# Scale sums in 64 columns and one bank, scaled rows on two engines, and the first tile's row products ahead of the constants' rows

## The chip, the cores and the metric

The kernel runs on one core of one Trainium2 chip. The metric is the device time of one execution in microseconds (us); lower is better. The engines are called PE (matrix products), PEld (its weight loads), DVE (vector), ACT (activation), POOL (GpSimd) and SP (which issues most of the transfers here). PSUM is the memory that PE writes; the kernel cuts it into banks of 128 partitions by 512 fp32 numbers.

## The reference

One block of a spectral network on x of 2048 rows by 512 columns. The condition c gives six rows of 512 (`sa, ca, ga, sb, cb, gb`). The first half normalizes x, scales it by 1+ca, shifts it by sa, filters it in the frequency domain and adds it back; the second half does the same around two dense layers with a Mish between.

```python
mod = (_silu(c) @ w_mod).reshape(c.shape[0], 6, 1, -1)
sa, ca, ga, sb, cb, gb = (mod[:, 0], mod[:, 1], mod[:, 2], mod[:, 3], mod[:, 4], mod[:, 5])
h = _layernorm(x, axis=-1) * (1 + ca) + sa
x = x + ga * _A_ref(h, A_w_r, A_w_i)    # irfft2(rfft2(h) * (w_r + 1j*w_i))
h = _layernorm(x, axis=-1) * (1 + cb) + sb
x = x + gb * _B_ref(h, B_w1, B_b1, B_w2)    # mish(h @ w1 + b1) @ w2
```

## The kernel before

The transform is written as matrix products with constant matrices. x is cut into 16 tiles of 128 rows. The first stage, which the change touches, runs over these tiles n = 0 to 15 and takes about the first 49 us:

- `p1_row(n)`, the row products: four matmuls of the turned tile (`xring`, x with rows and columns exchanged, loaded by `load_xt`) with `krs`, the constant matrix `kr` whose rows are multiplied by 1+ca. So krs carries the scale of the norm, and no row product can start before ca is known.
- `row_sums()`: the same four matmuls with a matrix of ones instead of x. Their result, copied by ACT to `kb`, is what a row's mean has to be multiplied with. These are the constants' rows of the title.
- `norm_sums(n)` on DVE reads the tile itself (`x`, loaded by `load_x`) and gives mean and variance; `first_guess` on ACT (an Ln, L188, and an Exp, L189) and `first_scale` on DVE (three small instructions, L196) make 1/sqrt(variance) of them.
- `p1_mean(n)` on DVE (L284) takes mean times kb from the row products; `p1_cast` on ACT (L300 or L294) scales the result and rounds it to `gh`; `p1_low` on DVE (L307) makes the rest `gl` for even n (POOL does it for odd n).
- `p1_col(n)`: nine matmuls (three times L314, L315, L316) with `mring`, the column matrices that ACT and POOL split from `mraw` (`p1_split`, loaded by `load_m`). The last three of them take gl.

Ahead of this stands the prologue. `sc` is silu(c), spread over partitions. `scale_sums` makes ca: 16 matmuls, four steps k by four column blocks j, each with a 128x128 block of `wmc` (the part of w_mod for ca, loaded in four transfers, one for each k) as weights and one column of sc, repeated, as the moving operand. Each fp32 matmul runs as two passes, each with its weight load, so 16 matmuls show as 32 rows of PE and of PEld. Block j adds up in its own bank `ps[j]`, all columns of it alike. `scale_rows` is one DVE instruction for each block: krs[j] = kr[j] * ps[j] + kr[j]. A few matmuls on ones (`warm`, L355) run before the first load has landed.

In this stretch everything is issued in the order in which it is written (`manual_schedule`); each engine works through its own queue in that order, and waits on semaphores for the others. SP issues the loads one by one in the order written; with eight lanes, the ninth load waits until the first has landed, and so on. The later stages (spectral products, way back, dense layers in seven products in the order of a table) follow unchanged.

```python
def row_products(pg, data):                                          # L266
    pgv = pg.rearrange("p (c d q) -> p d c q", c=2, d=4)
    for j in range(4):
        nc.tensor.matmul(pgv[:, j], data(j), krs[:, j, :].rearrange("p (c q) -> p c q", c=2),
                         start=True, stop=True)                      # L269

def row_sums():                                                      # L277
    ps = bank("D")
    row_products(ps, lambda j: ones)
    nc.scalar.copy(kb, ps)                                           # L280

def p1_mean(n):                                                      # L282
    c = st.pop(("pg", n))
    nc.vector.scalar_tensor_tensor(c, kb, mv[:, n, 0:1], c, op0=ALU.mult, op1=ALU.subtract)
    st["c", n] = c
```

Of the kernel before, what the change touches and what calls it, by code (L numbers as in the profile page):

```python
# [7 lines left out]
F32 = mybir.dt.float32  # L8
F32R = mybir.dt.float32r
AF = mybir.ActivationFunctionType  # L10
ALU = mybir.AluOpType

P = 128
# [70 lines left out]
def tile_spectral_block(ctx: ExitStack, tc: tile.TileContext, x_d, w1_d, b1_d, w2_d,  # L84
                        c_d, xt_d, wm_d, wq_d, wz_d, kr_d, km_d, kc_d, ki_d, kf_d, kv_d, kw_d, kp_d, out_d):
    nc = tc.nc
# [4 lines left out]
    small = ctx.enter_context(tc.tile_pool(name="small", bufs=4))  # L91
# [21 lines left out]
    def bank(tag):  # L113
        return psum.tile([P, 512], F32, name="bank", tag=tag)
# [8 lines left out]
    def buf(tag, dt=F32):  # L123
        if tag in "ty":
            uses[tag] = uses.get(tag, 1) + 1
            return wide(tag)[:, uses[tag] % 2]
        return work.tile([P, 512], dt, name="buf", tag=tag)

    def plain(t):
        return t.bitcast(F32)  # L130

    x = base.tile([P, N2, D], F32, name="x")
    sc = base.tile([P, 4], F32, name="sc")
# [6 lines left out]
    krs = modr[:, 0].rearrange("p (j e) -> p j e", j=4)  # L140
# [11 lines left out]
    wmc = big.tile([P, 4, 512], F32, name="wmc", tag="cr")  # L152
# [8 lines left out]
    kr = pw.tile([P, 4, P], F32, name="kr")  # L161
# [6 lines left out]
    def scale_spread():  # L168
        ps = bank("D")
        for k in range(4):  # L170
            nc.tensor.matmul(ps[:, k * P:(k + 1) * P], sc[:, k:k + 1].to_broadcast([P, P]), ident,
                             start=True, stop=True)
        st["scb"] = ps
# [7 lines left out]
    def norm_sums(n):  # L181
        t = small.tile([P, 6], F32, name="st")
        nc.vector.bn_stats(t, x[:, n, :])
        nc.vector.bn_aggr(mv[:, n, :], t)
# [6 lines left out]
    def norm_refine(lo, hi, sign, r=None):  # L191
        r = rstd[:, lo:hi] if r is None else r
        t = small.tile([P, 4], F32, name="ve")[:, 0:hi - lo]
        for out, a, one, op in ((t, mv[:, lo:hi, 1], EPS, ALU.add), (t, t, -0.5 * sign, ALU.mult),
                                (rstd[:, lo:hi], t, 1.5 * sign, ALU.add)):
            nc.vector.scalar_tensor_tensor(out, a, one, r, op0=op, op1=ALU.mult)  # L196

    def first_guess(lo, hi):
        st["r", lo] = r = bank("D")[:, 0:hi - lo]
        norm_guess(lo, hi, r)  # L200

    def first_scale(lo, hi):
        norm_refine(lo, hi, -1, st.pop(("r", lo)))
# [27 lines left out]
    def load_m(n):  # L231
        nc.sync.dma_start(mraw[:, n, :], km_d[:, n, :])

    def load_x(n):
        nc.sync.dma_start(x[:, n:n + 1, :], xv[:, n:n + 1, :])

    def load_xt(n):
        t = xring[:, n % 8]
        nc.sync.dma_start(t, xt_d[n])
        st["xt", n] = t  # L240

    def load_all(n):
        load_xt(n)
        load_x(n)
        load_m(n)
# [13 lines left out]
    def p1_split(n):  # L259
        m = mt(n)  # L260
        nc.scalar.copy(m[:, 0, 0:256], mraw[:, n, :])
        nc.gpsimd.tensor_tensor(m[:, 1, 0:256], mraw[:, n, :], plain(m[:, 0, 0:256]), op=ALU.subtract)
        nc.gpsimd.tensor_scalar(m[:, :, 256:384], plain(m[:, :, 128:256]), -1.0, 0.0,
                                op0=ALU.mult, op1=ALU.add)
# [7 lines that stand above are left out]
    def p1_row(n):  # L272
        xt = st.pop(("xt", n))
        st["pg", n] = pg = bank("AB"[n % 2])
        row_products(pg, lambda j: xt[:, j, :])
# [11 lines that stand above are left out]
    def p1_cast(n):  # L287
        c = st["c", n]
        one = rstd[:, n:n + 1]
        gh, gl = buf("g1", F32R), buf("g2", F32R)  # L290
        if n in POOL_LOW:
            g = buf("t")
            if n == 1:
                nc.scalar.activation(gh, c, AF.Copy, scale=one)  # L294
            nc.scalar.activation(g, c, AF.Copy, scale=one)
            if n > 1:
                nc.scalar.copy(gh, g)
            nc.gpsimd.tensor_tensor(gl, g, plain(gh), op=ALU.subtract)
        else:
            nc.scalar.activation(gh, c, AF.Copy, scale=one)  # L300
        st["g", n] = gh, gl
# [17 lines left out]
    def p1_save(n):  # L319
        nc.scalar.copy(a_sb[:, :, n, :], st.pop(("pa", n)).rearrange("p (e q) -> p q e", e=8))  # L320

    def scale_sums(ks, ps):
        for k in ks:
            for j in range(4):
                nc.tensor.matmul(ps[j][:, 0:P], wmc[:, k, j * P:(j + 1) * P], sc[:, k:k + 1].to_broadcast([P, P]),  # L325
                                 start=(k == 0), stop=(k == 3))

    def scale_rows(ps):
        for j in range(4):
            nc.vector.scalar_tensor_tensor(krs[:, j, :], kr[:, j, :], ps[j][:, 0:1], kr[:, j, :],  # L330
                                           op0=ALU.mult, op1=ALU.add)

    def shift_sum(k):
        mod_column(wms[:, k, :], cols[:, 0, 0, k:k + 1], 128.0, bank("D"))
# [17 lines left out]
    def warm(count, tag="B"):  # L352
        ps = bank(tag)
        for _ in range(count):
            nc.tensor.matmul(ps[:, 0:P], ones, ones, start=True, stop=True)  # L355

    with tc.manual_schedule():
        nc.sync.dma_start(sc, c_d.rearrange("b (p k) -> p (b k)", k=4))
        nc.scalar.preload_act_table_set("natural_log_exp_and_others")
        for k in range(4):  # L360
            nc.sync.dma_start(wmc[:, k, :], wm_d[1, k])
        nc.sync.dma_start(kr, kr_d)
        load_x(0)
        load_xt(0)
        nc.sync.dma_start(ident, kp_d)
        load_xt(1)
        load_m(0)
        for n in range(1, 8):
            load_x(n)
            if n < 7:  # L370
                load_xt(n + 1)
            load_m(n)
        nc.vector.memset(ones, 1.0)
        nc.vector.memset(eps, EPS)
        nc.vector.memset(b1n[:, NF - 1:NF], 0.0)
        sg = small.tile([P, 4], F32, name="sg")
        nc.scalar.activation(sg, sc, AF.Exp, scale=-1.0)
        nc.vector.tensor_scalar(sg, sg, 1.0, None, op0=ALU.add)
        nc.vector.reciprocal(sg, sg)
        nc.vector.tensor_tensor(sc, sc, sg, op=ALU.mult)  # L380
        warm(6)
        cps = [bank(t) for t in "CCBB"]
        for k in range(4):
            scale_sums((k,), cps)
        scale_rows(cps)
        row_sums()
        norm_sums(0)
        first_guess(0, 1)
        first_scale(0, 1)
        p1_split(0)  # L390
        p1_row(0)
        load_all(8)
        p1_row(1)
        load_all(9)
        scale_spread()
        p1_mean(0)
        p1_cast(0)
        norm_sums(1)
        first_guess(1, 2)
        p1_split(1)  # L400
        nc.scalar.copy(scb, st.pop("scb"))
        p1_low(0)
        p1_mean(1)
        first_scale(1, 2)
        p1_split(2)
        p1_cast(1)
        norm_sums(2)
        for n in range(N2):
            if n >= 1 and n != 2:
                p1_save(n - 1)  # L410
            if n + 2 < N2:
                p1_row(n + 2)
                if n == 2:
                    p1_col(1, range(2, 3))
                    p1_save(1)
                if n + 10 < N2:
                    load_all(n + 10)
                if n == 4:
                    nc.sync.dma_start(wms, wm_d[0].rearrange("k p e -> p k e"))
                if n == 6:  # L420
                    load_rest()
            if 1 <= n and n + 1 < N2:
                p1_mean(n + 1)
                if n % 2:
                    first_scale(n + 1, n + 3)
                p1_cast(n + 1)
            for i in range(n + 2 + (n > 5), min(n + 3 + (n > 4), N2)) if n else ():
                p1_split(i)
            if n:
                p1_low(n)  # L430
            p1_col(n, range(2) if n == 1 else range(3))
            if n + 3 < N2:
                norm_sums(n + 3)
                if n % 2 == 0:
                    first_guess(n + 2, n + 4)
            if 11 <= n < 15:
                shift_sum(n - 11)
        p1_save(N2 - 1)
        shift_rows()
# [846 lines left out]
    start = {}  # L1286
# [232 lines left out]
```

## Time and profile before

| what | value |
|---|---|
| median of 3 runs | 367.63 us (367.11 to 368.03) |
| the profiled execution's own time | 368.36 us |
| its span (first to last instruction) | 366.6 us |
| mean granted clock of PE | 0.997 |
| PE busy | 358.6 us, 98% |
| DVE busy | 302.5 us, 83% |
| ACT busy | 266.9 us, 73% |
| POOL busy | 78.3 us, 21% |

All times of a trace are counted from the start of its span. The profiled execution took 1.8 us more than its span and 0.7 us more than the median. A PE that is nearly always busy says that work on PE sets the time as long as nothing keeps it waiting; what a change of the prologue does is read from the first 20 us alone.

### The profile page before, as it was taken

What the parts mean: (1) busy time and instruction counts of PE and PEld (TensorE: products, weight loads), DVE (VectorE), ACT (ScalarE), POOL (GpSimd) and SP (SyncE); (2) the same over time, 40 slices, a digit from 0 to 9 for tenths busy, and PEclk for the clock granted to TensorE, in tenths of its full rate; (3) what the DMA queues carried; (4) which work ended last, traced back from release to release, by engine and by line L of the source; (5) the groups of instructions that cost most, each with busy time, mean ns of one, the idle gap of its engine ahead of it and who ended that gap; (6) DMA issues with size and microseconds to landing.
All of it is one profiled execution on the core that took longest, in us unless ns stands there. A gap on an engine that the chain in (4) does not pass through costs nothing.

```text
span 366.6 us, 7820 instructions
## 1 busy us (share of the span) xinstructions
PE 358.6 (98%) x2666; PEld 333.9 (91%) x2666; DVE 302.5 (83%) x752; ACT 266.9 (73%) x601; POOL 78.3 (21%) x126
## 2 busy tenths in 40 slices
PE   8999999998999999999999999999999999999994
PEld 8999977777999998798999999999999999999994
DVE  1898968888889799998994777998759977887995
ACT  1798879996799999998773878766577753555650
POOL 0588738786011001100002101004100000000000
PEclk9999999999999999999999999999999999999998
DMA  7999997678498776899888877786989678863133
GB/s 254 383 349 377 331 373 250 219 185 305 142 327 254 236 256 230 278 306 322 248 225 292 276 236 200 207 276 206 281 301 243 215 229 266 227 219 62 59 57 115
DMA packets 54343, 89.96 MB, mean 245 GB/s; under 512 B 7552, under 2 KB 20960, under 8 KB 54048
## 3 DMA queue, kind: packets, MB, share of 16 engines
q1 hardware_dynamic: 49728, 74.65, 62.0%
q0 software_dynamic: 2416, 7.87, 9.0%
q10 hardware_dynamic: 2160, 6.95, 6.0%
q8 instruction: 21, 0.34, 0.4%
q14 instruction: 18, 0.15, 0.1%
HBM read 68.21 MB, written 17.57 MB: 234 GB/s over the span
## 4 chain that ended last, share of the span: by engine, by line
PE 84%; ACT 5%; DVE 4%; DMA 2%; POOL 1%; issue 1%; ACTq 1%; SPq 0%; DVEq 0%; POOLq 0%
PE bank L1091 25%; PE bank L991 22%; PE bank L974 6%; PE bank L269 4%; PE bank L869 4%; PE bank L859 3%; PE bank L860 3%; PE bank L1037 3%; PE bank L314 3%; PE bank L1087 3%; DMA hT<-in_B_w_dram 2%; PE bank L1103 2%; PE bank L316 1%; PE bank L315 1%; PE bank L325 1%
## 5 line engine op out<-in xcount | busy, mean ns | idle before, releaser
L991 PE MATMUL bank<-hT,wr 128*128 128x256 f32 x360 | 51.6, 283 | 0.0
L991 PEld LDWEIGHTS bank<-hT,wr 128*128 128x128 f32 x360 | 47.3, 191 | 0.6
L991 PE MATMUL bank<-hB,wr 128*128 128x256 f32 x318 | 46.6, 285 | 0.0
L991 PEld LDWEIGHTS bank<-hB,wr 128*128 128x128 f32 x318 | 41.9, 191 | 0.9
L1143 POOL DMA_DIRECT2D x<-modr x7 | 6.3, 898 | 140.5 <-DVE modr L1142 84.7
L1091 PE MATMUL bank<-w2a,ah 128*128 128x256 f32 x161 | 35.1, 283 | 0.0
L917 DVE TENSOR_TENSOR al<-buf,ah 128x512 fp32r<-128x512 f32 (+1 forms) x45 | 30.1, 668 | 5.7 <-ACT ah L916 4.7
L1091 PE MATMUL bank<-w2b,ah 128*128 128x256 f32 x147 | 32.2, 283 | 0.0
L916 ACT CAST ah<-buf 128x512 fp32r<-128x512 f32 (+1 forms) x45 | 27.0, 602 | 4.5 <-DVE buf L1061 2.6
L1091 PEld LDWEIGHTS bank<-w2a,ah 128*128 128x128 f32 x161 | 27.0, 191 | 0.4
L859 PE MATMUL bank<-kc,d 128*128 128x128 f32 x128 | 24.9, 276 | 0.5 <-ACT d L452 0.5
L1091 PEld LDWEIGHTS bank<-w2b,ah 128*128 128x128 f32 x147 | 24.9, 191 | 0.3
L860 PE MATMUL bank<-kc,d 128*128 128x128 f32 x128 | 24.8, 275 | 0.0
L974 PE MATMUL bank<-hB,wr 128*128 128x512 f32 x96 | 24.4, 393 | 0.0
L1091 PE MATMUL bank<-w,ah 128*128 128x256 f32 x112 | 21.5, 284 | 0.0
L314 PE MATMUL bank<-buf,mring 128*128 128x512 f32 x48 | 20.6, 430 | 0.2 <-DVE buf L307 0.2
L974 PEld LDWEIGHTS bank<-hB,wr 128*128 128x128 f32 x96 | 17.3, 189 | 3.1
L859 PEld LDWEIGHTS bank<-kc,d 128*128 128x128 f32 x128 | 19.4, 192 | 0.7 <-ACT d L452 0.7
L860 PEld LDWEIGHTS bank<-kc,d 128*128 128x128 f32 x128 | 19.5, 192 | 0.0
L1091 PEld LDWEIGHTS bank<-w,ah 128*128 128x128 f32 x112 | 17.7, 191 | 0.6
L608 PEld LDWEIGHTS bank<-kv,a_sb 128*128 128x128 f32 x126 | 15.5, 192 | 2.8 <-issue 2.2
L788 POOL DMA_DIRECT2D turned<-x x16 | 8.9, 568 | 42.1 <-DVE x L782 42.1
(310 smaller groups left out, 1098.2 us busy)
## 6 DMA issues: line engine op xcount, KB each, us to landing
wr<-w_S SPq DMA_DIRECT2D x60, 256.0 KB, 4.0
wr<-w_A SPq DMA_DIRECT2D x45, 256.0 KB, 3.8
w_S<-hT SPq DMA_DIRECT2D x20, 256.0 KB, 2.9
x<-in_A_x_dram SPq DMA_DIRECT2D x16, 256.0 KB, 4.7
xring<-in_x_t_dram SPq DMA_DIRECT2D x16, 256.0 KB, 4.6
w_A<-wr SPq DMA_DIRECT2D x15, 256.0 KB, 3.1
x<-modr POOLq DMA_DIRECT2D x7, 512.0 KB, 5.5
out_dram<-x SPq DMA_DIRECT2D x7, 512.0 KB, 3.8
```

What stands on the lines that cost most here:

```text
L269: nc.tensor.matmul(pgv[:, j], data(j), krs[:, j, :].rearrange("p (c q) -> p c q", c=2), start=True, stop=True)
L314: nc.tensor.matmul(pa, m[:, a, 0:128], g, start=(i == 0), stop=False)
L608: nc.tensor.matmul(pd[:, i * P:(i + 1) * P], y[:, i * P:(i + 1) * P], kv[:, 0:128], start=True, stop=True)
L859: nc.tensor.matmul(o, dj[:, 0:128], kc[0][:, n, :], start=True, stop=False)
L860: nc.tensor.matmul(o, dj[:, 64:192], kc[1][:, n, :], start=False, stop=True)
L869: nc.tensor.matmul(px[:, j * P:(j + 1) * P], e[:, j * P:(j + 1) * P], kiv[:, j, :], start=True, stop=True)
L916: nc.scalar.copy(h, r)
L917: nc.vector.tensor_tensor(l, r, plain(h), op=ALU.subtract)
L974: nc.tensor.matmul(ups[i, t, f], ring[t, a][:, p, b, :], sides[int(a[2]) - 1][:, :, q, b, :], start=(a[2] == "1" and b == 0 and n == 0), s ...
L991: nc.tensor.matmul(o, w[:, p, k, :], h[:, q, k, :], start=(first and n == 0), stop=(last and n == 5), skip_group_check=True)
L1037: nc.tensor.matmul(ups[i, 0][:FL], w1s[:, p, u, :], sides[u // 2][:, :, q, u % 2, :], start=(u == 0 and p + q == 0), stop=(u == 3 and p == ...
L1091: nc.tensor.matmul(out_ps[b][n][:, 256 * half:256 * half + 256], a[p][:, e], w2[t][q][:, r], start=(t == 1 and half == 0 and i == 0), stop ...
```

## The change

Four edits, all ahead of the second tile:

1. `scale_sums` uses 64 repeated columns instead of 128, and the four blocks j share one bank, 64 columns each (the accumulation flag is set only at the first of them).
2. `scale_rows` first makes `one` = 1 + sums, a 128x4 tile, with one DVE instruction for all four blocks, and then multiplies kr[j] by it: blocks 0 and 2 on DVE, 1 and 3 on ACT.
3. SP loads the first turned tile ahead of the first tile of x; `load_m(0)` and `load_xt(1)` move ahead of `ident`.
4. `p1_row(0)` stands ahead of `row_sums()`, and `first_scale(0, 1)` behind `p1_mean(0)`.

```diff
-    def scale_sums(ks, ps):
-        for k in ks:
-            for j in range(4):
-                nc.tensor.matmul(ps[j][:, 0:P], wmc[:, k, j * P:(j + 1) * P], sc[:, k:k + 1].to_broadcast([P, P]),
-                                 start=(k == 0), stop=(k == 3))
+    def scale_sums(k, ps):
+        for j in range(4):
+            nc.tensor.matmul(ps[:, 64 * j:64 * j + 64], wmc[:, k, j * P:(j + 1) * P], sc[:, k:k + 1].to_broadcast([P, 64]),
+                             start=(k == 0 and j == 0), stop=(k == 3), skip_group_check=True)
 
     def scale_rows(ps):
-        for j in range(4):
-            nc.vector.scalar_tensor_tensor(krs[:, j, :], kr[:, j, :], ps[j][:, 0:1], kr[:, j, :],
-                                           op0=ALU.mult, op1=ALU.add)
+        one = small.tile([P, 4], F32, name="one")
+        nc.vector.tensor_scalar(one, ps[:, 0:256:64], 1.0, None, op0=ALU.add)
+        for j in range(0, 4, 2):
+            nc.vector.tensor_scalar(krs[:, j, :], kr[:, j, :], one[:, j:j + 1], None, op0=ALU.mult)
+            nc.scalar.activation(krs[:, j + 1, :], kr[:, j + 1, :], AF.Copy, scale=one[:, j + 1:j + 2])
...
         nc.sync.dma_start(kr, kr_d)
+        load_xt(0)
         load_x(0)
-        load_xt(0)
+        load_m(0)
+        load_xt(1)
         nc.sync.dma_start(ident, kp_d)
-        load_xt(1)
-        load_m(0)
...
         warm(6)
-        cps = [bank(t) for t in "CCBB"]
+        cps = bank("C")
         for k in range(4):
-            scale_sums((k,), cps)
+            scale_sums(k, cps)
         scale_rows(cps)
+        p1_row(0)
         row_sums()
         norm_sums(0)
         first_guess(0, 1)
-        first_scale(0, 1)
         p1_split(0)
-        p1_row(0)
         load_all(8)
         p1_row(1)
         load_all(9)
         scale_spread()
         p1_mean(0)
+        first_scale(0, 1)
         p1_cast(0)
```

The instructions on PE from the program's start, before (`bank` is any PSUM tile, `modr` holds krs, `xring` the turned tiles; L171 is `scale_spread`):

```order
L355 MATMUL bank<-ones 128x128 x6
L325 MATMUL bank<-sc,wmc 128x128 x16
L269 MATMUL bank<-modr,ones 128x2x64 x4
L269 MATMUL bank<-modr,xring 128x2x64 x8
L171 MATMUL bank<-ident,sc 128x128 x4
L269 MATMUL bank<-modr,xring 128x2x64 x4
```

and now:

```order
L356 MATMUL bank<-ones 128x128 x6
L324 MATMUL bank<-sc,wmc 128x64 x16
L269 MATMUL bank<-modr,xring 128x2x64 x4
L269 MATMUL bank<-modr,ones 128x2x64 x4
L269 MATMUL bank<-modr,xring 128x2x64 x4
L171 MATMUL bank<-ident,sc 128x128 x4
L269 MATMUL bank<-modr,xring 128x2x64 x4
```

The matmuls are the same in number; the four on ones have moved behind the first four on xring.

The instructions on DVE behind silu(c), before (`modr` of L330 is krs, L183 and L184 are `norm_sums(0)`, L284 is `p1_mean(0)`):

```order
L330 SCALAR_TENSOR_TENSOR modr<-kr,bank 128x128 x4
L183 BN_STATS st<-x 128x6
L184 BN_AGGR mv<-st 128x2
L196 SCALAR_TENSOR_TENSOR ve<-mv,bank 128x1
L196 SCALAR_TENSOR_TENSOR ve<-ve,bank 128x1
L196 SCALAR_TENSOR_TENSOR rstd<-ve,bank 128x1
L284 SCALAR_TENSOR_TENSOR bank<-modr,mv,bank 128x512
L183 BN_STATS st<-x 128x6
```

and now:

```order
L329 TENSOR_SCALAR one<-bank 128x4
L331 TENSOR_SCALAR modr<-kr,one 128x128 x2
L183 BN_STATS st<-x 128x6
L184 BN_AGGR mv<-st 128x2
L284 SCALAR_TENSOR_TENSOR bank<-modr,mv,bank 128x512
L196 SCALAR_TENSOR_TENSOR ve<-mv,bank 128x1
L196 SCALAR_TENSOR_TENSOR ve<-ve,bank 128x1
L196 SCALAR_TENSOR_TENSOR rstd<-ve,bank 128x1
L183 BN_STATS st<-x 128x6
```

Two of the four large instructions have left for ACT, a small one stands ahead of them, and L284 has moved ahead of the three of L196.

## The prediction

> **What bounds the kernel now.** I read the page first, then the windows of the first stage, the chain of waits in its first 20 us, and the timelines of DVE, ACT and PE there. PE is busy nearly throughout:
>
> ```profile
> PE 358.6 (98%) x2666; PEld 333.9 (91%) x2666; DVE 302.5 (83%) x752; ACT 266.9 (73%) x601; POOL 78.3 (21%) x126
> ```
>
> So a delay ahead of the main work is paid in full unless something later was waiting anyway. The windows (time, then busy us of PE, PEld, DVE, ACT, POOL) show where the first stage changes its limit:
>
> ```profile
> 8.60:13.10 4.50, 4.50 (x41) 4.50 (x40) 3.63 (x12) 2.13 (x6) 1.12 (x2) 1.00 1.06 387
> 13.10:19.60 6.50, 6.32 (x44) 5.47 (x42) 6.26 (x18) 5.63 (x14) 4.53 (x7) 1.00 1.06 380
> 19.60:49.00 29.40, 29.39 (x211) 27.27 (x212) 26.60 (x68) 24.82 (x57) 22.15 (x31) 1.00 1.02 348
> ```
>
> From 19.6 us on PE never stands still. Before that PE and DVE are both nearly full, and which of them is last is told by the chain of waits, and by the waits of PEld from 8 to 50 us:
>
> ```profile
> 1.18 2.90 DMA wmc<-in_w_mod_dram
> 4.21 4.53 PE bank L325 x32
> ...
> 18.74 0.75 DVE buf L307
> ...
> 19.54 0.50 PE bank L314
> ```
>
> ```profile
> PEld bank L314 <- DVE buf L307: 0.6, 2, 0.4
> ```
>
> At 19.54 PE gets gl of tile 2 from DVE, up to 0.4 us late; it is the last wait before the stage where PE alone decides. So I ask of each edit when DVE ends that L307. The timeline of DVE:
>
> ```profile
> 8.11 1.16 DVE L330 SCALAR_TENSOR_TENSOR modr<-kr,bank 128x128 f32<-128x128 f32 x4 [4.87 <-PE bank L325]
> ...
> 10.82 0.15 DVE L196 SCALAR_TENSOR_TENSOR ve<-mv,bank 128x1 f32<-128x1 f32 x1 [0.73 <-ACT bank L189]
> ...
> 11.27 0.75 DVE L284 SCALAR_TENSOR_TENSOR bank<-modr,mv,bank 128x512 f32<-128x512 f32 x1
> 11.93 0.69 DVE L183 BATCH_NORM_STATS2 st<-x 128x6 f32<-128x512 f32 x1
> ...
> 18.74 0.74 DVE L307 SCALAR_TENSOR_TENSOR buf<-bank,rstd,buf 128x512 fp32r<-128x512 f32 x1
> ```
>
> The last wait of DVE that is marked is the 0.73 us ahead of 10.82. From there to 19.48 it works without a pause (6.26 of 6.5 us in the window, the rest being steps between small dependent instructions). The change keeps all this work and exchanges only its first pieces, L196 and L284. So the rule for the sum: **whatever moves the start of that stretch, 10.82 us, moves the end.** It hangs on ACT, and ACT on the end of the row sums on PE:
>
> ```profile
> 9.85 0.58 ACT L280 COPY modr<-bank 128x512 f32<-128x512 f32 x1 [7.22 <-PE bank L269]
> 10.33 0.27 ACT L188 ACTIVATE bank<-mv,eps 128x1 f32<-128x1 f32 x1
> 10.63 0.16 ACT L189 ACTIVATE bank<-bank 128x1 f32<-128x1 f32 x1
> ```
>
> ```profile
> 8.58 1.23 PE L269 MATMUL bank<-modr,ones 128*128 128x128 f32 x8
> 9.65 1.95 PE L269 MATMUL bank<-modr,xring 128*128 128x128 f32 x16
> ```
>
> Row sums end 9.82 (8.58+1.23), copy to kb, Ln, Exp, then DVE at 10.82: 1.00 us behind the row sums.
>
> **64 columns.** The passes of the sums, first at the low clock and then at the high one, and the weight loads by their number of weight columns (last numbers: min/median/max ns, or mean ns):
>
> ```profile
> 4.56 1.06 PE L325 MATMUL bank<-sc,wmc 128*128 128x128 f32 x4
> 6.24 2.28 PE L325 MATMUL bank<-sc,wmc 128*128 128x128 f32 x19
> L325 PE MATMUL bank<-sc,wmc x24: 273/274/275, 5.8 to 8.4; 128*128 128x128 f32 x24
> L325 PEld LDWEIGHTS bank<-sc,wmc x23: 190/191/192, 5.9 to 8.4; 128*128 128x128 f32 x23
> L476 PEld LDWEIGHTS bank<-kf,early 128*1 128x1 f32 x2 | 0.1, 82 | 0.2 <-issue 0.2
> L1037 PEld LDWEIGHTS bank<-hB,w1s 128*96 128x96 f32 x48 | 7.4, 162 | 2.0
> L559 PE MATMUL bank<-early,kf 128*128 128x384 f32 x2 | 0.8, 487 | 0.0
> ```
>
> A pass starts (2.28-0.274)/18 = 0.111 us behind the one before, at the low clock (1.06-0.42)/3 = 0.213. The array needs (487-274)/256 = 0.83 ns a column, so 0.107 us for 128 columns and 0.053 for 64. The load needs 82 ns for one weight column, 162 for 96, 191 for 128: 0.86 ns a weight column, 0.11 us for 128. Every pass has its own load of 128 weight columns, and the change leaves those. So in the pass of 0.111 us both halves are full, and halving one leaves the other: I take the pitch at 0.111 us, with 0.056 (the array alone) as the other end. [...]
>
> At equal pitch the sums end where they did. But DVE's first krs needed only block 0 and could start at 8.11. The single instruction `one` reads all four blocks, so it waits for the last of 32 passes: it starts at 8.47 as before (4.21+4.53-0.274, the chain's row of L325) and lasts 0.274-0.053 = 0.22, end 8.69, DVE at 8.73. **+0.62.**
>
> **Rows on two engines.** Rows nearest to the new instructions:
>
> ```profile
> 2.66 0.17 DVE L378 TENSOR_SCALAR sg<-sg 128x4 f32<-128x4 f32 x1 [1.66 <-ACT sg L377]
> 2.87 0.18 DVE L379 RECIPROCAL sg<-sg 128x4 f32<-128x4 f32 x1
> L456 DVE TENSOR_SCALAR d<-bank 128x128 f32<-128x128 f32 x9 | 2.6, 284 | 0.5 <-ACT d L452 0.5
> L454 ACT ACTIVATE d<-bank 128x128 f32<-128x128 f32 x8 | 2.4, 297 | 0.0
> ```
>
> `one` is like L378, 0.17, with the next dependent instruction 0.21 behind (2.66 to 2.87). Then krs 0 on DVE: 0.28 at most by L456, which reads PSUM; 0.18 by L379 at least; I take 0.24. Before, one instruction of 0.35 did this: from the start on DVE to krs 0 **+0.10** (bounds 0.04 to 0.14). ACT, which idled 7.22 us there, makes krs 1 meanwhile, from 0.23 behind `one` in some 0.3 to 0.4 us, in time for PE's second matmul. In return the eight passes no longer wait for DVE: from 8.58 to the start of the next group they took 1.07 (9.65), eight passes alone take 0.89, of which I leave 0.05 to the load ahead of the first: **-0.13.**
>
> **Row products first.** Eight passes now stand ahead of the row sums, 8 x 0.111: **+0.89** on the end of the row sums and on kb. Row products of tile 0 themselves come earlier, but nobody waits for them: L284 needs kb too.
>
> **first_scale behind p1_mean.** DVE now starts its stretch with L284, which needs kb but neither Ln nor Exp: 0.03 to ACT, copy 0.58, 0.04 to DVE, 0.66 behind the row sums instead of 1.00: **-0.34.** Ln and Exp end 0.36 behind the copy, covered by L284 (0.66 until the next can start). What is queued behind the moved L284 is all of DVE's stretch, and PE waits for that at 19.54.
>
> **Loads.**
>
> ```profile
> 3.53 0.43 SPq L235 DMA_DIRECT2D x<-in_A_x_dram  x1
> 4.00 0.43 SPq L239 DMA_DIRECT2D xring<-in_x_t_dram  x1
> x<-in_A_x_dram SPq DMA_DIRECT2D x1, 256.0 KB, 4.6
> xring<-in_x_t_dram SPq DMA_DIRECT2D x1, 256.0 KB, 4.8
> 5.43 0.43 SPq L232 DMA_DIRECT2D mraw<-in_km_dram  x1
> mraw<-in_km_dram SPq DMA_DIRECT2D x1, 128.0 KB, 4.6
> ```
>
> The first tile landed at 8.1 and its turned form at 8.8; they change places, equal in size. Row products start at 9.3 in the new order, so neither is waited for; the norm sums of tile 0 have until kb, 11.9, and need 0.9 from 8.8. The other three exchange places among themselves and are all there by 10.0 (5.43+4.6); their readers, PE's next row products and ACT's split, come behind 11. SP issues each 0.47 behind the last without a wait, so no later load moves. Nothing.
>
> **Sum.** 0.62+0.10-0.13+0.89-0.34 = **+1.14 us** on the start of DVE's stretch, 11.96, with bounds of about 0.95 to 1.35 from the small terms. PE's own way is later by less (0.62+0.10 at the first row product, -0.13), and at 19.54 it waits. The profiled execution of 368.36 would become 369.5; its distance to the median is no part of the change, so 367.63+1.14 = **368.8 us.** That is 0.31%, just about the 0.3% that a measurement of this kernel can tell from no change.
>
> **The rivals.** *Narrow passes are shorter* (not slower). For it: a load of 128 weight columns need not take 191 ns:
>
> ```profile
> L539 PEld LDWEIGHTS bank<-ident,a_sb 128*128 128x128 f32 x63 | 7.5, 141 | 7.0 <-issue 4.0 <-DVE early L542 0.8 <-ACT buf L591 0.7
> ```
>
> Those are transposes. At 0.056 us the sums would be bound by the last wmc:
>
> ```profile
> 1.18 1.84 SPq L361 DMA_DIRECT2D wmc<-in_w_mod_dram  x4
> wmc<-in_w_mod_dram SPq DMA_DIRECT2D x1, 256.0 KB, 4.2
> ```
>
> It is issued at 2.6 and lands at 6.8; eight passes more and `one` could start at 7.5, krs 0 be done at 7.95; but the turned tile lands at 8.1, so PE starts row products at 8.3 and the row sums end at 8.3+15x0.111+0.28 = 10.25, L284 at 10.9: +0.1, 367.7. At 0.08, halfway, `one` starts at 7.75, the row products at 8.4: +0.2. It decides from a pitch below 0.1. Where the clock steps up later than in this trace (at the low clock a pass costs 0.102 more, now half of that), it gains, up to some 0.7: 367.0.
>
> *The clock rises later* (slower).
>
> ```profile
> 1.04 2.93 PE L355 MATMUL bank<-ones 128*128 128x128 f32 x12 [1.04 <-DVE b1n L375]
> ```
>
> The passes went from 0.213 to 0.111 at 5.6 us, 4.6 behind the first matmul at 1.0. If the lighter passes don't count as enough work, and the step comes as long behind the first sum at 4.2, at 8.8, some 14 passes more run at the low clock, 14 x 0.102 = 1.4: 370.2. Against it: PE's loads stay as dense. [...]
>
> *The chain through DVE is not the last*: then PE's own +0.6 stays, 368.2. The wait at 19.54 speaks against it.
>
> **How the numbers follow.** Forecast 0.68; narrow passes shorter 0.22; later clock 0.08; PE's own way 0.02. Of the forecast's bounds (0.95 to 1.35) rather more than half lies above the 1.1 us that are 0.3%: slower 0.42+0.08 = 0.50. Faster needs short passes and a late clock step, or a spread like that of the three runs (0.9 us): 0.07. The rest, 0.43, is the same. The range leaves out the late clock and the best of the short passes: 367.3 to 369.5.
>
> **What would show it.** Right: passes of the new sums still 0.11 us apart; DVE's `one` at about 8.7; L284 of tile 0 at about 11.9, without a further pause of DVE up to its L307 near 19.9; PE's last wait near 20.7. Wrong: passes 0.06 to 0.08 apart and `one` before 8; L284 before 11; or passes 0.2 apart beyond 6 us.

## The result and the profile after

| | before | after |
|---|---|---|
| median of 4 runs | 367.83 us (367.11 to 368.44) | 373.06 us (371.99 to 373.58) |
| profiled execution / its span | 368.36 / 366.6 us | 373.03 / 371.3 us |

The ratio of after to before is 1.0139 (95% interval 1.011 to 1.0169): 5.2 us slower. The forecast was 368.8 with a range up to 369.5, so the direction was right and the size was not: the experiments below give the forecast's own sum some 1.1 of the 5.2 us, and the rest to a cause that the sum had left out.

The page of after, top and busy times. PE has gained 4.5 us of busy time on the same 2666 instructions; it waited hardly more (8.2 us of the span instead of 8.0), its instructions got longer:

```profile
span 371.3 us, 7821 instructions
PE 363.1 (98%) x2666; PEld 338.4 (91%) x2666; DVE 302.0 (81%) x751; ACT 267.5 (72%) x603; POOL 78.4 (21%) x126
```

Where they got longer is seen in the timeline of after (start, duration, engine, line, what, how many; in brackets the idle time before and what ended it):

```profile
1.04 2.93 PE L356 MATMUL bank<-ones 128*128 128x128 f32 x12 [1.04 <-DVE b1n L376]
...
4.06 6.90 PEld L324 LDWEIGHTS bank<-sc,wmc 128*128 128x128 f32 x32 [0.39 <-issue]
4.09 7.06 PE L324 MATMUL bank<-sc,wmc 128*128 128x64 f32 x32
...
11.19 0.16 DVE L329 TENSOR_SCALAR one<-bank 128x4 f32<-128x4 f32 x1 [7.99 <-PE bank L324]
...
11.73 2.08 PE L269 MATMUL bank<-modr,xring 128*128 128x128 f32 x8 [0.58 <-DVE modr L331]
...
13.60 1.92 PE L269 MATMUL bank<-modr,ones 128*128 128x128 f32 x8
15.30 1.59 PE L269 MATMUL bank<-modr,xring 128*128 128x128 f32 x8
...
16.16 0.76 DVE L284 SCALAR_TENSOR_TENSOR bank<-modr,mv,bank 128x512 f32<-128x512 f32 x1 [3.48 <-ACT modr L280]
16.73 1.06 PE L171 MATMUL bank<-ident,sc 128*128 128x128 f32 x8
...
24.87 0.50 PE L314 MATMUL bank<-buf,mring 128*128 128x512 f32 x1 [0.18 <-DVE buf L307]
```

One line's instructions (min/median/max ns, first and last start):

```profile
L324 PE MATMUL bank<-sc,wmc x32: 421/421/445, 4.1 to 10.7; 128*128 128x64 f32 x32
```

All 32 passes of the sums stand (7.06-0.421)/31 = 0.214 us apart, each reported at 421 ns, which is the pace of the first passes before. Before, only those ahead of 5.7 us had it. The low clock holds on: the first 16 passes of L269 take 2.08 and 1.92 us for eight, where eight at the high clock take 1.06 (the row of L171). Only in the third group, from 15.30 on, does the pace change, at about 16.4 us instead of 5.7.

That this pace is a low clock needs a word, because a row of the windows seems to say otherwise (time; busy us of PE, PEld, DVE, ACT, POOL; granted clock; DMA share; GB/s):

```profile
6.20:9.60 3.40, 3.40 (x18) 3.40 (x18) 0.00 (x0) 0.00 (x0) 0.00 (x0) 1.00 1.04 377
```

Eighteen passes of PE fall into these 3.4 us; into the 3.4 us from 16.5 on fall 29. The trace's record of the granted clock has its first entry only at the rise: 5.73 us behind the span's start in the kernel before, 16.41 in this one. For the time ahead of it the views print 1.00 for want of an entry, so the table's 0.997 of the kernel before leaves out its first microseconds as well. Where the record does hold a low stretch, in the tenth kernel below, it has 0.50, and eight passes take 2.08 us there as they do here.

Against the forecast, `one` starts at 11.19 instead of 8.73 (+2.46), and from `one` to L284 it takes 4.97 instead of 3.23 (+1.74, of which 16 passes by 0.102 are 1.63). With the +1.14 forecast that makes 5.34 on the start of DVE's stretch: 10.82 before, 16.16 now. PE's last wait for gl moves from 19.54 to 24.87, by 5.33. Further on a little is given back. The waits of PEld from 90 to 105 us before, the instruction behind the second of them in the timeline of before, and the waits of that stage after:

```profile
PEld bank L859 <- ACT d L452: 0.7, 1, 0.7
PEld bank L869 <- ACT buf L862: 0.5, 1, 0.5
```

```profile
97.77 1.16 PE L869 MATMUL bank<-kiv,buf 128*128 128x128 f32 x8 [0.35 <-ACT buf L862]
```

```profile
PEld bank L860 <- ACT d L453: 0.7, 1, 0.7
```

The wait of 0.5 us for ACT at 97.77 is gone, since ACT did not come later by as much as PE: its L862 starts at 97.16 before and at 101.83 after (L863 there), 4.67 us later. So the span is 4.7 us longer, not 5.3.

### The profile page after: what moved, and what is told of

Same layout as the page of the kernel before. It is cut to its first block, busy times and chain, and to the rows that moved or that the text cites. A ratio compares the mean times of both kernels' runs of the same rounds, so it can differ in the third digit from the quotient of the medians.

```text
span 371.3 us, 7821 instructions
## 1 busy us (share of the span) xinstructions
PE 363.1 (98%) x2666; PEld 338.4 (91%) x2666; DVE 302.0 (81%) x751; ACT 267.5 (72%) x603; POOL 78.4 (21%) x126
## 4 chain that ended last, share of the span: by engine, by line
PE 84%; ACT 5%; DVE 5%; DMA 2%; issue 1%; POOL 1%; SPq 1%; ACTq 0%; DVEq 0%
PE bank L1092 25%; PE bank L992 22%; PE bank L975 6%; PE bank L860 4%; PE bank L870 4%; PE bank L861 4%; PE bank L269 4%; PE bank L1038 3%; PE bank L314 3%; PE bank L1088 3%; PE bank L1104 1%; PE bank L315 1%; PE bank L316 1%; DMA kr<-in_kr_dram 1%; PE bank L560 1%
## 5 line engine op out<-in xcount | busy, mean ns | idle before, releaser
L269 PE MATMUL bank<-modr,xring 128*128 128x128 f32 x128 | 18.4, 291 | 0.6 <-DVE modr L331 0.6
```

## The experiments

The passes did not become shorter, as forecast, and yet the clock rose 10.7 us later. **Theory A**: the clock rises after a stretch of some 3.4 us (the tenth kernel's record, below, has windows of 3.413 us between its steps) in which columns move through the array nearly all the time; a pass of 64 columns moves them half the time, since the load of 128 weight columns sets its pitch (0.214 us here, 0.213 with 128 columns before). **Theory B**: the changed order, or PE's pause ahead of the row products, holds the clock down. A2, later, is a variant of A: what counts is how much of the array works, and not only how long columns move. The kernel before ran beside each group: 368.19 (first four), 367.97 (next four), 367.96 (last three).

**128 columns, everything else as after**

```diff
-  matmul(ps[:, 64*j:64*j+64],    ..., sc[:, k:k+1].to_broadcast([P, 64]))     # one reads ps[:, 0:256:64]
+  matmul(ps[:, 128*j:128*j+128], ..., sc[:, k:k+1].to_broadcast([P, 128]))    # one reads ps[:, 0:512:128]
```

> The changed kernel with 128 columns again, still in one bank and with all its other edits. Theory A (the narrow matmuls keep the clock of PE low: their array time is half of a pass, and that is too little work for the clock to rise): passes go from 0.213 to 0.111 us near 5.6 us as in the kernel before, DVE's `one` starts near 8.7, and the time is the prediction's sum, about 1.1 us over the kernel before (369.0). Theory B (the clock stays low because PE pauses between sums and row products, or because of the new order): the clock rises as late as in the changed kernel, near 16 us, and the time stays near 373.

Measured: 369.1 us (368.15 to 369.9, ten runs), ratio 1.0030 (1.0018 to 1.0043). Two answers on L324 (from 4 to 6.6 us, and from 6.7 us on) and the timeline:

```profile
L324 PE MATMUL bank<-sc,wmc x12: 374/421/551, 4.1 to 6.6; 128*128 128x128 f32 x12
L324 PE MATMUL bank<-sc,wmc x22: 273/273/421, 6.4 to 8.9; 128*128 128x128 f32 x22
```

```profile
9.24 0.16 DVE L329 TENSOR_SCALAR one<-bank 128x4 f32<-128x4 f32 x1 [6.04 <-PE bank L324]
...
9.78 1.16 PE L269 MATMUL bank<-modr,xring 128*128 128x128 f32 x8 [0.58 <-DVE modr L331]
10.78 1.06 PE L269 MATMUL bank<-modr,ones 128*128 128x128 f32 x8
...
12.49 0.76 DVE L284 SCALAR_TENSOR_TENSOR bank<-modr,mv,bank 128x512 f32<-128x512 f32 x1 [1.75 <-ACT modr L280]
```

The step is back in the sums, at 6.8 us. The number of columns alone is worth some 4 of the 5.2 us, and B is wrong: the new order with its pause stands here too. What is left, +1.1 us (0.7 to 1.6), is the forecast's sum of 1.14, and from `one` to L284 it takes 3.25 us, forecast 3.23. `one` itself is later than 8.73 because in this execution the step came 1 us later than in the one of before, some five passes by 0.102.

**64 columns alone, in the kernel before**

```diff
-  matmul(ps[j][:, 0:P],  ..., sc[:, k:k+1].to_broadcast([P, P]))
+  matmul(ps[j][:, 0:64], ..., sc[:, k:k+1].to_broadcast([P, 64]))
```

> The kernel before with only the columns of the sums cut from 128 to 64 (four banks, DVE rows, order and loads as before). Theory A: the passes stay at 0.213 us until some 4 us of the full row products have run, the sums end near 11 us instead of 8.5, and the time is 4 to 5 us over the kernel before (about 372). Theory B: the clock rises near 5.6 us and the time is the same as before within 0.3 us.

Measured: 370.92 us (ten runs: eight from 370.27 to 371.85, two at 367.66 and 367.81), ratio 1.0062 (1.0034 to 1.0089). The line of the sums and the row sums behind them:

```profile
L325 PE MATMUL bank<-sc,wmc x32: 421/421/447, 4.0 to 10.6; 128*128 128x64 f32 x32
```

```profile
10.83 2.02 PE L269 MATMUL bank<-modr,ones 128*128 128x128 f32 x8
```

With nothing of the other three edits the clock stays low through the sums and the row sums. It costs less here (+2.7, where 4 to 5 were expected) because DVE still starts its krs block by block and only eight row passes stand in the way of kb.

**96 columns**

```diff
-  matmul(ps[:, 64*j:64*j+64], ..., sc[:, k:k+1].to_broadcast([P, 64]))
+  matmul(ps[:, 96*j:96*j+96], ..., sc[:, k:k+1].to_broadcast([P, 96]))
```

> The changed kernel with 96 columns: array time three quarters of a pass at the pitch that the weight load sets. Theory A: the pitch stays 0.213 at the low clock and 0.111 at the high one; the clock rises either near 5.6 us (time about 369.0) or late (about 373), by whether three quarters are enough; no time between except by one step of the clock. Theory B: about 373.

Measured: 370.77 us (370.67 to 371.09, four runs), ratio 1.0079 (1.0063 to 1.0094). The sums in its timeline, and the line's passes from 4 to 10 us and from 10.3 us on:

```profile
4.26 6.63 PE L324 MATMUL bank<-sc,wmc 128*128 128x96 f32 x32 [0.29 <-DMA wmc<-in_w_mod_dram]
```

```profile
L324 PE MATMUL bank<-sc,wmc x27: 421/421/500, 4.3 to 9.9; 128*128 128x96 f32 x27
L324 PE MATMUL bank<-sc,wmc x6: 275/275/421, 9.9 to 10.6; 128*128 128x96 f32 x6
```

The step comes at 10.2, between the other two. In the 3.4 us before it columns moved 96/128 = 75% of the time; in the 3.4 us before those some 66% (0.35 us of full warm passes, a pause of 0.50, the rest at 75%), and the clock did not rise.

**A longer warm-up, 64 columns as after**

```diff
-        warm(6)
+        warm(16)
```

> The changed kernel (64 columns) with 16 instead of 6 full matmuls on ones ahead of the sums, so that PE works densely from 1.0 to about 6.8 us and the clock has risen before the narrow matmuls begin. Theory A, with the weight load as the limit of a pass: the narrow passes then run 0.111 us apart at the high clock, not 0.056, the sums take 3.6 us and end near 10.5, and the rest runs at the high clock: 2.9 us later than a kernel whose `one` starts at 8.7, so about 371.0 to 372.0, below the changed kernel. If the array were the limit, the passes would be 0.056 apart and the sums would end near 8.8: about 369.3. Theory B: the clock falls or stays low around the pause, 373 or more.

Measured: 370.8 us, one execution. Its timeline, and one line's loads:

```profile
1.04 6.04 PE L356 MATMUL bank<-ones 128*128 128x128 f32 x32 [1.04 <-DVE b1n L376]
6.92 3.68 PE L324 MATMUL bank<-sc,wmc 128*128 128x64 f32 x32
10.64 0.16 DVE L329 TENSOR_SCALAR one<-bank 128x4 f32<-128x4 f32 x1 [7.43 <-PE bank L324]
```

```profile
L324 PEld LDWEIGHTS bank<-sc,wmc x32: 192/192/192, 6.8 to 10.3; 128*128 128x128 f32 x32
```

Now the 64-column passes run wholly at the high clock (the record has the rise at 5.69): (3.68-0.275)/31 = 0.110 us apart. That settles the prediction's first question, which the result alone could not: at the high clock too the weight load set the pitch, 0.110 us against 0.111 with 128 columns before, and 64 columns gained nothing. The 2.8 us by which the sums start later (6.92 instead of 4.09) are what this cure costs.

**Half the weight columns in each load**

```diff
+            for h in (0, 64):
-                nc.tensor.matmul(ps[:, 64*j:64*j+64],      wmc[:, k, j*P:(j+1)*P],       ...)
+                nc.tensor.matmul(ps[h:h+64, 64*j:64*j+64], wmc[:, k, j*P+h:j*P+h+64],    ...)
```

> The changed kernel (64 columns) with each weight block of 128 columns cut into two of 64, so 32 matmuls in 64 passes: each pass loads 64 weight columns and moves 64, and half of the array's columns are used. The load then needs half the time, and the moving columns fill the whole pass again. Theory A (the clock follows the share of time in which columns move through the array): passes of 0.107 us at the low clock, the step near 4.5 to 7 us, passes of 0.056 behind it, and a time as with 128 columns, about 369. Theory A2 (it follows the amount of work, so the narrow form itself holds it low): passes of 0.107 throughout, the sums still end near 11, the clock rises behind 12, and the time is 371 to 373.

Measured: 370.52 us (six runs: 368.08 and 368.29, four from 370.19 to 371.29), ratio 1.0054 (1.0029 to 1.008). The profiled execution was the one of 368.08:

```profile
4.35 2.04 PE L325 MATMUL bank<-sc,wmc 128*64 128x64 f32 x48 [0.38 <-DMA wmc<-in_w_mod_dram]
...
6.79 0.69 PE L325 MATMUL bank<-sc,wmc 128*64 128x64 f32 x16 [0.41 <-DMA wmc<-in_w_mod_dram]
7.53 0.16 DVE L331 TENSOR_SCALAR one<-bank 128x4 f32<-128x4 f32 x1 [4.33 <-PE bank L325]
...
8.48 1.13 PE L269 MATMUL bank<-modr,xring 128*128 128x128 f32 x8 [1.00 <-DMA xring<-in_x_t_dram]
```

Sixteen passes of 64 weight and 64 moving columns take 0.69 us; eight whole ones take 1.06. With half the weight columns in each load the narrow passes do get shorter, so it was the load that set their pitch: here passes start (0.69-0.22)/15 = 0.031 us apart on average, where the passes with whole loads stand 0.110 apart at this clock (the fourth run). The sums end with the last wmc, `one` comes at 7.53, and the row products then wait for the turned tile, as the prediction's first rival had it for short passes. Why four of the six took 2 to 3 us longer this trace does not show. The profiled execution of the tenth kernel, below, shows one way, a fall of the clock after its first rise. Three of the four would fit it: their mean granted clocks are 0.988, 0.994 and 0.994, that of the tenth kernel's execution is 0.994, and the two short ones here have 1.000 and 0.999. The fourth long one has 0.999, and stays unexplained.

**128 columns and the order of before** (one bank, rows on two engines and the loads stay as after)

```diff
         scale_rows(cps)
-        p1_row(0)
         row_sums()
         norm_sums(0)
         first_guess(0, 1)
+        first_scale(0, 1)
         p1_split(0)
+        p1_row(0)
...
         p1_mean(0)
-        first_scale(0, 1)
```

> The changed kernel with 128 columns and the old order of row sums, row products and first_scale (edit 4 undone), with one bank, rows on two engines and the new loads kept. By the prediction's terms 0.62+0.10-0.13 = +0.6 us over the kernel before remain, against +1.1 with the new order. Rival: the new order costs nothing (it only swaps eight passes for eight): then it stays at +1.1.

Measured: 368.87 us (367.86 to 371.56, twelve runs), ratio 1.0032 (1.0016 to 1.0049). The runs spread too widely to tell 0.6 from 1.1 in the total. The trace (368.65) does tell it:

```profile
9.03 0.16 DVE L329 TENSOR_SCALAR one<-bank 128x4 f32<-128x4 f32 x1 [5.68 <-PE bank L324]
...
11.74 0.15 DVE L196 SCALAR_TENSOR_TENSOR ve<-mv,bank 128x1 f32<-128x1 f32 x1 [1.20 <-ACT bank L189]
```

From `one` to the first of DVE's stretch 2.71 us, as from L330 to L196 before (8.11 to 10.82), against 3.25 with the new order. The forecast's terms for the two engines, +0.10 and -0.13, cancel there as well.

**The order alone, in the kernel before**: the third and the fourth edit, with 128 columns in four banks and `scale_rows` of before.

```diff
-        load_x(0); load_xt(0); load ident; load_xt(1); load_m(0)
+        load_xt(0); load_x(0); load_m(0); load_xt(1); load ident
...
         scale_rows(cps)
+        p1_row(0)
         row_sums()
...
-        first_scale(0, 1)
...
-        p1_row(0)
...
         p1_mean(0)
+        first_scale(0, 1)
```

> The kernel before with edits 3 and 4 alone (loads and order), 128 columns in four banks and rows on DVE as before. By the prediction's terms 0.89-0.34 = +0.55 us over the kernel before; the first row product cannot start before the turned tile has landed near 8.2, which is before krs is there, so the loads add nothing. Rival: the order costs nothing and L284 starts near 10.8 as L196 did before: +0.0.

Measured: 368.78 us (368.4 to 369.1, eleven runs), ratio 1.0021 (1.0013 to 1.003), +0.8 us (0.5 to 1.1).

```profile
8.60 1.16 DVE L330 SCALAR_TENSOR_TENSOR modr<-kr,bank 128x128 f32<-128x128 f32 x4 [5.40 <-PE bank L325]
...
11.85 0.75 DVE L284 SCALAR_TENSOR_TENSOR bank<-modr,mv,bank 128x512 f32<-128x512 f32 x1 [1.27 <-ACT modr L280]
```

3.25 us instead of 2.71: +0.54, where the terms +0.89 and -0.34 make 0.55.

**Only the good half of the order**: `first_scale` behind `p1_mean`, and one warm matmul more, in the kernel before.

```diff
-        warm(6)
+        warm(7)
...
-        first_scale(0, 1)
...
         p1_mean(0)
+        first_scale(0, 1)
```

> The kernel before with first_scale behind p1_mean, but with the row sums still ahead of the row products, and with 7 instead of 6 full matmuls on ones, which fill the pause of PE ahead of the first sums. DVE's stretch starts with L284, which needs the copy (10.43) and the row products of tile 0 (10.7): near 10.75 instead of 10.82, so 0.0 to 0.1 us less; the seventh matmul may let the clock rise at an earlier window in some executions, which is worth up to 0.5 us in those. Together 0.0 to 0.4 us less than the kernel before, at the edge of what can be told.

Measured: 368.24 us (367.71 to 368.84, eleven runs), ratio 1.0008 (0.9997 to 1.0019). No gain.

```profile
7.73 1.16 DVE L330 SCALAR_TENSOR_TENSOR modr<-kr,bank 128x128 f32<-128x128 f32 x4 [4.53 <-PE bank L325]
...
9.27 1.95 PE L269 MATMUL bank<-modr,xring 128*128 128x128 f32 x16
...
10.42 0.76 DVE L284 SCALAR_TENSOR_TENSOR bank<-modr,mv,bank 128x512 f32<-128x512 f32 x1 [0.71 <-ACT bank L189]
```

From L330 to L284 2.69 us: the stretch starts no earlier than before (2.71 to L196), where -0.34 alone would give 2.37. With the row sums first, the row products that L284 needs end about 10.3 (9.27+0.28+7x0.111), as late as ACT's Exp, to which the wait is put down. So the -0.34 is not to be had without the row products first, which cost the +0.89.

**The half loads again**, the same kernel as the fifth, for a trace in which the clock rises at another moment.

> The half loads once more, for a profile of one of the longer executions: of six, two took 368.1 to 368.3 and four 370.2 to 371.3, and the profile showed one of the two, in which the clock had risen at 4.7 us, while mostly full matmuls had run. Theory A (share of time with moving columns): in a longer execution, too, the clock rises by 8 us, and the time went elsewhere. Theory A2 (amount of work; half of the array is not enough): pairs of passes stay near 0.117 us apart, the sums end near 8, the row products run at the low clock to 11 us or later. If this execution is again a short one, it tells nothing.

Measured: 368.51 us. Its sums in the timeline, and the line's passes from 4 to 6.7 us and from 6.8 us on:

```profile
4.31 2.72 PE L325 MATMUL bank<-sc,wmc 128*64 128x64 f32 x48 [0.34 <-DMA wmc<-in_w_mod_dram]
```

```profile
L325 PE MATMUL bank<-sc,wmc x45: 264/314/370, 4.3 to 6.7; 128*64 128x64 f32 x45
L325 PE MATMUL bank<-sc,wmc x23: 220/220/314, 6.5 to 8.0; 128*64 128x64 f32 x23
```

Here the clock rose at about 6.8 us, and most of the 3.4 us before it were passes of 64 weight by 64 moving columns. As they stand twice as dense as after's, columns moved some 83% of that time (what is missing is mostly the pause of 0.55 us ahead of them, 3.76 to 4.31). So narrow passes as such did not hold the clock down. A2 is not settled by it: the passes come in pairs, one on each half of the weight columns, which run side by side (45 passes between 4.3 and 6.7 us, a pair every 0.107 us, just what 64 columns need at the low clock, 0.213/2), and so the whole array was at work. No run here tells A from A2. And since this execution was a short one, it does not show what the long ones did.

**Half loads with the order of before**: the fifth kernel, but with the loads and the row sums in the order of before, and `warm(8)`, in the hope of a kernel faster than both. `first_scale` stays behind `p1_mean`.

```diff
-        warm(6)
+        warm(8)
...
         scale_rows(cps)
-        p1_row(0)
         row_sums()
...
         p1_split(0)
+        p1_row(0)
```

> A version meant to beat both: half loads in one bank, rows on two engines, row sums still ahead of the row products, first_scale behind p1_mean, the loads in the old order, and 8 full matmuls on ones ahead. With the clock up at 5 us the sums end with the last load of wmc near 7.4, the row sums end near 9.3, L284 starts near 10.3 when the row products of tile 0 are there, 0.5 us ahead of the kernel before. By theory A the clock is up by 8 us at the latest: 367.4 to 368.0, against 368.0 before. By theory A2 the eight full matmuls (to 4.5 us) make an early rise likelier than the half loads alone had it, but not sure: a median of 367.5 with some executions 2 to 3 us longer.

Measured: 368.05 us (367.42 to 370.24, thirteen runs), ratio 0.9998 (0.9983 to 1.0012): the same as before. The profiled execution was the longest, and it shows the clock at work. Its timeline, and its windows (time; busy us of PE, PEld, DVE, ACT, POOL; granted clock; DMA share; GB/s):

```profile
6.71 0.69 PE L325 MATMUL bank<-sc,wmc 128*64 128x64 f32 x16 [0.26 <-DMA wmc<-in_w_mod_dram]
8.31 0.69 PE L325 MATMUL bank<-sc,wmc 128*64 128x64 f32 x16 [0.91 <-DMA wmc<-in_w_mod_dram]
...
9.58 2.08 PE L269 MATMUL bank<-modr,ones 128*128 128x128 f32 x8 [0.59 <-DVE modr L333]
```

```profile
6.10:9.40 3.30, 1.72 (x44) 1.31 (x40) 0.33 (x2) 0.16 (x1) 0.00 (x0) 1.00 1.01 339
9.40:12.80 3.40, 3.22 (x15) 3.22 (x16) 1.12 (x4) 1.61 (x6) 0.00 (x0) 0.50 0.99 336
12.80:14.00 1.20, 1.20 (x12) 1.20 (x12) 0.73 (x2) 0.14 (x1) 0.89 (x2) 0.99 1.00 302
```

The last wmc landed late. From 6.1 to 9.4 us PE had half its time to do (1.72 of 3.30), and the clock fell to 0.50 (in the record at 9.41); it stayed there for 3.4 us of dense row products and rose again: the record has 3.413 us at full clock from 6.00, 3.413 at half, and then full clock again. What share of such a window has to be filled for a step it does not show.

**The same with warm matmuls in the gaps**

```diff
             scale_sums(k, cps)
+            warm(2 if k == 3 else 1)
```

> The same with full matmuls on ones put in the pauses of PE: one behind each of the first three steps of the sums and two behind the last. They cost nothing where PE waits for wmc or for krs. Theory A2: they make up enough work for a rise within about 8 us in all executions, so fewer or no long ones: 367.4 to 368.0 throughout. Theory A: no difference to the version without them.

Measured: 368.71 us (368.33 to 369.51, eleven runs), ratio 1.0021 (1.0009 to 1.0032). No run is as long as the longest before it, but the filling costs more than it saves:

```profile
7.32 0.49 PE L358 MATMUL bank<-ones 128*128 128x128 f32 x2
7.74 0.69 PE L325 MATMUL bank<-sc,wmc 128*64 128x64 f32 x16
...
9.51 0.16 DVE L331 TENSOR_SCALAR one<-bank 128x4 f32<-128x4 f32 x1 [6.30 <-PE bank L325]
```

`one` comes at 9.51, against 7.53 and 8.26 in the two traces of half loads without fills. In this trace PE waits for no `wmc` any more, and each of the fills behind the first three steps stands in the way of the next step. No version was faster than the kernel before.

The windows of 3.41 us that end with a step of the clock, and others counted from the step by 3.41 us at a time, with the share of the time in which columns moved. The shares are estimates, worked out from the starts of the passes: a column counts 1.67 ns at the low clock (0.213 us for 128) and 0.83 ns at the high one (0.107 us for 128, from the prediction's rows of 384 and 128 columns), a pause nothing. The reported end of a pass is no measure of it, since a pass of 128 columns at the low clock is reported at 0.421 us while the next starts 0.213 behind it.

| kernel, window in us | clock in it | share | clock behind it |
|---|---|---|---|
| before, 2.3 to 5.7 | low | 0.83 | rises |
| 128 columns, 3.4 to 6.8 | low | 0.86 | rises |
| 96 columns, 3.4 to 6.8 / to 10.2 | low | 0.66 / 0.75 | stays low / rises |
| 64 alone, 3.3 to 6.7 / to 10.2 / to 13.6 | low | 0.54 / 0.50 / 0.86 | low / low / rises |
| after, 2.8 to 6.2 / to 9.6 / to 13.0 / to 16.4 | low | 0.61 / 0.50 / 0.51 / 1.0 | low / low / low / rises |
| order alone, 0.3 to 3.7 / to 7.1 | low | 0.73 / 0.92 | low / rises |
| half loads (second trace), 3.4 to 6.8 | low | 0.83 | rises |
| half loads (second trace), 6.8 to 10.2 | high | 0.49 | stays high |
| long warm-up, 9.1 to 12.5 | high | 0.53 | stays high |
| half loads, warm(8), 6.0 to 9.4 | high | 0.36 | falls |

The working for after's first window: the last warm pass starts at 1.04+2.93-0.42 = 3.55 and its columns last until 3.76, so from 2.75 on there are 1.01 us in full; the ten narrow passes that start from 4.09 to 6.04 move columns for 0.107 us each, 1.07; 2.08 of 3.41 is 0.61.

The kernels before and with 128 columns show how loose the moment is even where the passes are full: 4.96 (`warm(7)`), 5.31 (order of before), 5.73 (before), 6.79 (128 columns) and 7.10 us (order alone). In all thirteen traces the stretch of full clock that lasts to the end of the work is a whole number of 3.413 us, 104, 105 or 106 of them, while its start lies differently from trace to trace. So in these traces the steps come only at the ends of windows of this length, and these windows don't start with the program.

## Why the prediction was wrong

- **What bounds it, and the rule for the sum**: right. The start of DVE's stretch moved by 5.34 us, the last wait of PE by 5.33, the median by 5.2.
- **"At equal pitch the sums end where they did"**: the premise, that the load of 128 weight columns sets the pitch, was right at both clocks (0.214 in after, 0.110 behind the long warm-up; the 0.11 us that the prediction has for a load holds for the high one). The step that failed is the one beside it, that the pitch is 0.111 from 5.6 us on. That took the moment of the clock step from the trace of before, as if it belonged to the place in the program, while the edit changed what brings it about. The step came at 16.41 us, 4 of the 5.2 us follow from it, and 128 columns in the changed kernel bring it back to 6.79.
- **"Against it: PE's loads stay as dense."** They did (6.90 us of PEld for 32 loads without a gap), and it was no argument. With the same loads 64 columns left the clock low until 16.41 us and 128 lifted it at 6.79: here a dense stream of loads did not lift the clock, moving columns did (how long they move, or how much of the array works, stays open). On that sentence the chance of 0.08 rested. The prediction had the two facts in hand, 0.107 us of array in a pass of 0.111 before, 0.053 after, and so half an idle array.
- **The rival's price**, 1.4 us, was too small as well: it let the step come at 8.8, inside the sums. Here three windows with a share of 0.50 to 0.61 went by without a step (the ends at 6.2, 9.6 and 13.0), 24 more passes of the sums ran slow (2.46 us), and 16 passes of the row products with them (1.74), which the rival did not count.
- **`one` (+0.62), two engines (+0.10, -0.13)**: with 128 columns they stand within a total of +1.1 us (0.7 to 1.6) and a path from `one` to L284 of 3.25 (3.23). Not measured singly. One piece of the +0.62 was a little too small: the last narrow pass is taken at 0.22 us and is reported at 0.275 at the high clock (fourth run). **Row products first (+0.89) and `first_scale` behind (-0.34)**: +0.54 in the trace of the order alone, forecast 0.55. **Loads**: nothing was waited for in after, as forecast. (The view of `mraw` puts ACT's wait ahead of L332 down to that load, but L332 starts at 11.38 together with DVE's L331, both behind `one`.)
- **The range** left out the late clock on purpose, with its chance of 0.08; it was what happened. The direction was right for the forecast's own reasons, which the 128 columns show at +1.1 us; the other 4 of the 5.2 us had no place in it.

Argued and not shown: that the two short executions of the 64-column kernel, and the long ones of the half loads, are the same windows lying differently. For the 64 columns the table can be used to estimate it: a window that ends between about 3.8 and 5.2 us would be three quarters full, of warm passes and of the first sums, and the clock would rise early. That is some four tenths of all positions, and two of ten runs were short; no trace caught one of them.

## What to carry to other kernels

A matmul whose weight load is longer than its moving columns gained nothing here from fewer columns, at either clock (0.214 us a pass at the low one, 0.110 at the high one), and in the first microseconds it lost 4 us: PE's clock rose here only behind windows in which columns moved 0.75 of the time or more (the table's estimates), so ahead of the step keep the passes wide, and price a prologue at both clocks. When an edit lightens the work before a step of the clock, the step's time in the old trace is not a constant of the program but a result of that work (5.73 us before, 16.41 after), and of where the windows happen to lie (4.96 to 7.10 us with full passes). And of two orders on a path, the one that puts an instruction ahead of a shared input (here kb) delays all who need that input; together with its counterpart, `first_scale` behind, that term was read from the trace to within 0.05 us (0.55 forecast, 0.54 measured).

## What the runs showed of the hardware that was not expected

- The share of moving columns that lifted the clock lay near three quarters of a 3.4 us window: 0.75 rose, 0.73 did not (an estimate from the rows of two kernels; from 0.83 up it always rose, up to 0.66 never). Once high, the clock fell behind a window with 0.36 (the tenth kernel) and stayed high behind windows with 0.49 and 0.53 (the ninth and the fourth run), a share that did not lift it (0.50 and 0.51 in after). So in these traces it took less to hold the clock up than to lift it.
- Two matmuls on the two halves of the weight columns run side by side: 16 passes of 64 by 64 in 0.69 us, under 0.07 us a pair behind the first, where the one pass of 128 weight columns that they replace took 0.110 (fourth run).
